# Two small setup tiles of a decode block, written by ScalarE copies instead of by GpSimd

## The chip, the cores and the metric

The kernel runs on one core of a Trainium2 chip. The metric is device time in microseconds (us) of one execution, the median of several. A core has TensorE (PE, matmuls; its weight loads are listed as PEld), VectorE (DVE), ScalarE (ACT), GpSimd (POOL), and SyncE (SP), which here only issues DMAs. The engines run side by side, each through its own list of instructions in order, and wait for each other on semaphores. DMAs are issued from SP's list and from ACT's list (the rows marked SPq and ACTq).

## The reference

One token (`x`, 1024 numbers) goes through a layernorm, then through two branches whose results are added to `x`: attention over the last 4096 positions of a key and value cache (32 query heads, 4 key/value heads of 128), and a second layernorm with a two-layer MLP of 3584 hidden units.

```python
xn = _layernorm(x)
q = (xn @ wq).reshape(B, Sq, Hq, Dh).transpose(0, 2, 1, 3)
k, v = last W=4096 positions of each cache, repeated 8 times over the heads
p = _softmax(einsum(q, k) * Dh ** -0.5)
A = einsum(p, v).reshape(B, Sq, Hq * Dh) @ wo
B = gelu(_layernorm(xn) @ w1 + b1) @ w2 + b2
return x + A + B
```

All inputs are bf16. With one token every matrix is read once and used for a matrix-vector product: 4 MB each of K, V (windows) and 8 MB each of wq and wo, some 7 MB each of w1 and w2, together close to 40 MB.

## The kernel before, in words

The order of the work on each engine follows from the program's order; a framework adds the semaphore waits that the tiles' reads and writes ask for.

**The stream of loads.** SP issues nearly all of them, in this order: the four K groups into the first half of the `big` tile `kq` (line 76), the two halves of wq (line 85), half of b1 (204), w1 (207), four V groups (214), w2 (220), and wo in five pieces (228), the last of them 256 KB. The tiles live in pools of two buffers each: `big` holds `kq`, `kt2`, `w1t`, `w2t` in turn, `ring` holds the second half of wq, `v_sb`, and the two halves of wo. So the load of w1 waits for the readers of `kq`, that of w2 for the readers of `kt2`, and the last four pieces of wo for the readers of `v_sb`. ACT issues four tiny loads at the start (108 to 111): `x` in two layouts, b2, and half of b1.

**Setup.** POOL fills constants: `zb` (line 91, bf16: an identity, one-hot selections `spread`, `sel_x`, `sel_b`, and room for the query), `ones_f`, `mhalf`, then `zf` (line 113, float32: 512 columns of zeros named `zeros`, a selection `sel4` of 32 columns, and two columns `sel01`), then `o8z` (116) and further selections, made by affine_select, which puts a one where an index expression is met. ACT copies the identity to float32 (`ident_f`, line 96), loads its exp table, issues the four tiny loads, and copies `zeros` into the accumulators in PSUM: `accf` (178) and the two halves of `accq` (182).

**Layernorms.** PE spreads `x` over 128 partitions with `spread` as weights (145). Each of the two layernorms is a chain: two ACT passes with sums (153, 154), one PE sum over partitions (156), one ACT scaling (158), five small POOL steps (160 to 167). The first gives `xnT` (173), the second `yT`.

**The middle.** DVE transposes K (191), DVE and ACT move its blocks (202, 200); PE makes q (237), the hidden layer (249), the scores (266) and the values' sum `o_all` (302).

**The end.** The final product adds 28 rows of w2 and 32 rows of wo. All but the last eight go to `accf` as single rows (329; for wo the weights are `o8z[:, c, 1:2]`, one column). ACT copies `accf` to `bulk` (333). Then two small accumulators `acct` collect the output in its final layout: first the bulk is moved over with selections as weights (342; one of the four selections is `sel01`, a 33x2 matrix whose only one stands in row 0, column 1), then the last eight rows of wo are added with two-column weights (348), of which one column is the attention output and the other must be zero: `o8z` has three columns a row, and `o8z[:, c, 1 - r:3 - r]` takes (value, zero) or (zero, value). Line 313 writes the middle column late; the outer two must hold zeros from the setup. `res` is put together by DVE (351) and ACT (352) and sent out by SP and ACT (354, 355).

In the listed program `tc.issue_after(instruction)` puts what is in its block behind that instruction in the engine's order.

Of the kernel before, what the change touches and what calls it, by code (L numbers as in the profile page):

```python
# [10 lines left out]
ALU = mybir.AluOpType  # L11
# [4 lines left out]
def kernel(  # L16
# [14 lines left out]
    nc = tc.nc  # L31
# [15 lines left out]
    CWO = NQ // P  # L47
# [34 lines left out]
    for i in range(2):  # L82
# [11 lines left out]
                            pattern=[[-1, P]], channel_multiplier=1)  # L94
    ident_f = consts.tile([P, P], FP32)
# [11 lines left out]
    with tc.issue_after(first_exp.ins):  # L107
# [5 lines left out]
    nc.gpsimd.memset(zf[:], 0.0)  # L113
    zeros = zf[:, 0:512]
    o8z = consts.tile([P, CWO, 3], BF16)
    nc.gpsimd.memset(o8z[:], 0.0)
    sel4 = zf[:, 512:512 + Hq]
    sel01 = zf[0:33, 512 + Hq:]
    nc.gpsimd.affine_select(out=sel01, in_=sel01, compare_op=ALU.not_equal, fill=1.0, base=-1,
                            pattern=[[1, 2]], channel_multiplier=2)  # L120
    qm_f = zb[:, P:P + 160]
    spread = zb[0:Hq, 288:800].rearrange("h (q p) -> h q p", q=4)
    sel_b = zb[0:8, 800:1056].rearrange("k (s m) -> k s m", s=2)
# [1 line left out]
    for sel, base in ((sel_x, 0), (sel_x, -64), (sel_b, 0)):  # L125
        nc.gpsimd.affine_select(out=sel, in_=sel, compare_op=ALU.not_equal, fill=1.0, base=base,
                                pattern=[[-16, 2], [-1, sel.shape[2]]], channel_multiplier=16)
    for R in range(4):
        nc.gpsimd.affine_select(out=sel4, in_=sel4, compare_op=ALU.not_equal, fill=1.0, base=-32 * R,
                                pattern=[[-1, Hq]], channel_multiplier=1)  # L130
# [3 lines left out]
                            pattern=[[-1, 4], [1, P]], channel_multiplier=-4)  # L134
# [4 lines left out]
                            pattern=[[-REP, Hkv]], channel_multiplier=1)  # L139
    nc.gpsimd.affine_select(out=gmask[:], in_=gmask[:], compare_op=ALU.is_ge, fill=0.0, base=REP - 1,  # L140
                            pattern=[[REP, Hkv]], channel_multiplier=-1)
# [38 lines left out]
    acch = ps_acc.tile([P, 2, 512], FP32, tag="acch", name="acch")  # L180
    for b in range(2):
        nc.scalar.copy(out=accq[:, b, :], in_=zeros)
    for s in range(2):
        nc.tensor.matmul(accf[0:64, 256 * s:256 * s + 256], lhsT=sel_x[:, s, :], rhs=xb8[:], start=(s == 0), stop=False)

# [46 lines left out]
    for i, w3 in enumerate(wq_tiles):  # L232
        for r in range(4):
            c = 4 * i + r
# [151 lines left out]
```

## Time and profile before

| what | value |
|---|---|
| three runs | 101.68, 101.80, 101.92 us; median 101.80 |
| the profiled execution's own time | 101.61 us |
| its span, first to last instruction | 99.5 us (so 2.1 us lie around it) |
| mean granted TensorE clock | 0.914 |
| busy: PE, DVE, ACT, POOL | 47.6, 37.5, 28.9, 8.9 us |
| moved by DMA | 39.91 MB, mean 401 GB/s over the span |

How to read it: busy times of engines are averages over stages with different limits, so they say little by themselves. The chain of waits goes back from the last instruction, at each step to what released it. In the timeline a row gives start, duration, engine and line, the tile written, an arrow, the tile read, and in brackets the idle time of that engine before it with what ended it. Lines over 356 belong to the wrapper that all engines run before and after the program.

### The profile page before, as it was taken

How to read it: one execution, taken by the hardware profiler on the slowest of the kernel's cores; microseconds unless marked ns; L12 is line 12 of the kernel's file. 1: busy time of each engine (PE TensorE's matmuls, PEld its weight loads, DVE VectorE, ACT ScalarE, POOL GpSimd, SP SyncE). 2: the span in 40 equal slices, each digit the busy share in tenths (PEclk: the TensorE clock that was granted, in tenths of full speed). 3: DMA queues.
4: the chain of work that ended last, by engine and by line, in shares of the span. 5: the costliest groups of instructions: out<-in, count | busy, mean ns of one | idle time of the engine just before them, and what ended most of it. 6: DMA issues, size and time to landing. Idle time of an engine off the chain costs nothing.

```text
span 99.5 us, 1001 instructions
## 1 busy us (share of the span) xinstructions
PE 47.6 (48%) x405; PEld 20.2 (20%) x405; DVE 37.5 (38%) x25; ACT 28.9 (29%) x32; POOL 8.9 (9%) x35
## 2 busy tenths in 40 slices
PE   0005110007600880089139807999100999895770
PEld 0003110002100310063036402334000333341240
DVE  0079999999999970010613015000600000000001
ACT  5306200007999999900150080000010000000201
POOL 7921560000000000000001000000000000000000
PEclk9999999999999999999999985579955558999999
DMA  2999999999999888999499999899899999899930
GB/s 46 389 409 435 484 428 474 474 422 422 448 422 581 369 369 369 392 669 415 181 425 422 435 576 392 369 576 491 369 392 418 422 422 422 362 441 408 394 114 1
DMA packets 2539, 39.91 MB, mean 401 GB/s; under 512 B 340, under 2 KB 360, under 8 KB 616
## 3 DMA queue, kind: packets, MB, share of 16 engines
q1 hardware_dynamic: 2460, 39.85, 93.9%
q8 instruction: 3, 0.05, 0.2%
q10 hardware_dynamic: 76, 0.01, 0.1%
HBM read 39.86 MB, written 0.00 MB: 401 GB/s over the span
## 4 chain that ended last, share of the span: by engine, by line
DMA 79%; PE 14%; SPq 3%; issue 1%; DVE 0%; DVEq 0%
DMA v_sb<-in_A_v_cache_dram 32%; DMA wo<-in_A_wo_dram 25%; DMA kq<-in_A_wq_dram 17%; PE o_all L302 10%; DMA kq<-in_A_k_cache_dram 5%; PE accq L237 4%; SPq L214 1%; SPq L228 1%; SPq L207 0%; PE acct L348 0%; DVE res L351 0%; DVEq L351 0%
## 5 line engine op out<-in xcount | busy, mean ns | idle before, releaser
L200 ACT COPY kt<-kt 32x4096 bf16<-32x4096 bf16 x5 | 18.0, 3601 | 10.2 <-DVE kt L191 10.2
L191 DVE STREAM_TRANSPOSE kt<-kq 128x4096 bf16<-128x4096 bf16 x4 | 17.4, 4413 | 5.6 <-DMA kq<-in_A_k_cache_dram 5.6
L202 DVE COPY kt<-kt 32x4096 bf16<-32x4096 bf16 x11 | 13.4, 1218 | 0.2
L302 PE MATMUL o_all<-v_sb,w1t 128*32 128x512 bf16 x32 | 9.8, 480 | 3.4 <-DMA v_sb<-in_A_v_cache_dram 3.4
L329 PE MATMUL accf<-w2t 128*1 128x512 bf16 x56 | 8.9, 496 | 4.8 <-DMA w2t<-in_B_w_dram 4.8
L351 DVE TENSOR_TENSOR res<-acct,bulk 34x120 bf16<-34x120 f32 x1 | 0.3, 275 | 25.1 <-PE acct L348 25.1
L237 PE MATMUL accq<-kq,xnT 128*1 128x512 bf16 x32 | 3.6, 625 | 10.2 <-DMA kq<-in_A_wq_dram 10.2
L333 ACT COPY bulk<-accf 34x512 f32<-34x512 f32 x1 | 0.6, 579 | 20.9 <-PE accf L329 20.9
L237 PE MATMUL accq<-wq,xnT 128*1 128x512 bf16 x32 | 3.6, 627 | 6.1 <-DMA wq<-in_A_wq_dram 6.1
L329 PE MATMUL accf<-wo,o8z 128*1 128x512 bf16 x48 | 5.5, 379 | 1.6 <-DMA wo<-in_A_wo_dram 1.6
L237 PEld LDWEIGHTS <-xnT 128*1 128x1 bf16 x64 | 2.1, 115 | 20.6 <-issue 20.6
L302 PEld LDWEIGHTS <-w1t 128*32 128x32 bf16 x32 | 3.7, 117 | 9.4 <-issue 7.4
L329 PEld LDWEIGHTS <-w2t 128*1 128x1 bf16 x56 | 3.0, 103 | 10.3 <-issue 8.6
L249 PE MATMUL acch<-w1t,yT 128*1 128x448 bf16 x64 | 5.1, 488 | 0.0
L305 DVE TENSOR_TENSOR o_m<-o_all,grs 32x512 f32<-32x512 f32 x1 | 0.7, 679 | 9.1 <-PE o_all L302 9.1
L297 DVE STREAM_TRANSPOSE w2t<-w1t 128x896 bf16<-128x896 bf16 x1 | 1.7, 1702 | 6.2 <-ACT w1t L294 6.2
L145 PE MATMUL x_ps<-x,zb 32*128 32x8 bf16 x4 | 0.2, 163 | 7.9 <-DMA x<-in_A_x_dram 7.9
L309 ACT CAST o_bf<-o_f 32x128 bf16<-32x128 f32 x1 | 0.3, 297 | 12.6 <-DVE o_f L307 12.6
L266 PE MATMUL sp<-kt,zb 128*32 128x512 bf16 x32 | 3.7, 631 | 0.3 <-DVE zb L258 0.3
L253 PE MATMUL qT_ps<-zb,w1t 128*128 128x128 bf16 x8 | 1.0, 311 | 5.2 <-ACT w1t L239 5.2
L293 POOL TENSOR_SCALAR zcol<-l_loc 128x1 f32<-128x1 f32 x1 | 0.2, 238 | 36.9 <-ACT w1t L281 36.9
L249 PEld LDWEIGHTS <-yT 128*1 128x1 bf16 x64 | 3.1, 108 | 1.5
(80 smaller groups left out, 40.6 us busy)
## 6 DMA issues: line engine op xcount, KB each, us to landing
w1t<-in_B_w_dram SPq DMA_DIRECT2D x1, 7168.0 KB, 24.0
w2t<-in_B_w_dram SPq DMA_DIRECT2D x1, 7168.0 KB, 29.8
kq<-in_A_k_cache_dram SPq DMA_DIRECT2D x4, 1024.0 KB, 7.1
kq<-in_A_wq_dram SPq DMA_DIRECT2D x1, 4096.0 KB, 17.2
wq<-in_A_wq_dram SPq DMA_DIRECT2D x1, 4096.0 KB, 24.3
v_sb<-in_A_v_cache_dram SPq DMA_DIRECT2D x4, 1024.0 KB, 25.9
wo<-in_A_wo_dram SPq DMA_DIRECT2D x1, 4096.0 KB, 39.1
wo<-in_A_wo_dram SPq DMA_DIRECT2D x1, 2048.0 KB
```

The source lines that it names most:

```text
L191: nc.vector.transpose(out=scr[:, g, :], in_=k2[:, g, :])
L200: nc.scalar.copy(out=dst, in_=src)
L202: nc.vector.tensor_copy(out=dst, in_=src)
L214: nc.sync.dma_start(out=v4[:, g, :, :], in_=A_v_cache[0, g, Sk - W:Sk, :].rearrange("(p c) d -> p c d", p=P))
L228: nc.sync.dma_start(out=tv[:, a:b, :], in_=wo_v[:, nr * i + a:nr * i + b, :])
L237: nc.tensor.matmul(accq[32 * t:32 * t + 1, b, :], lhsT=xnT[:, c:c + 1], rhs=w3[:, r, j * 512:(j + 1) * 512], start=(c == 0), stop=(c == C ...
L249: nc.tensor.matmul(acch[32 * t:32 * t + 1, b, :NH], lhsT=yT[:, c:c + 1], rhs=w1v[:, c, j * NH:(j + 1) * NH], start=False, stop=(c == C - 1 ...
L253: nc.tensor.transpose(qT_ps[:, b * 4 + hh, :], q_sb[:, b, hh * Dh:(hh + 1) * Dh], ident)
L266: nc.tensor.matmul(sp[32 * R:32 * R + 32, a, :], lhsT=qm[:, g, :], rhs=kT[:, g, c0:c0 + 512], start=(g == 0), stop=(g == Hkv - 1), tile_po ...
L297: nc.vector.transpose(out=hT, in_=h_sb.rearrange("p (d c) -> p c d", c=CW2))
L302: nc.tensor.matmul(o_all[:].rearrange("h g d -> h (g d)"), lhsT=eTb[:, 32 * c:32 * c + 32], rhs=v4[:, :, c, :], start=(c == 0), stop=(c == ...
L329: last = nc.tensor.matmul(accf[32 * half:32 * half + 1, :], lhsT=vec[kind](c), rhs=wap[:, half * 512:(half + 1) * 512], start=False, stop= ...
```

## The change

Two GpSimd instructions go: the memset of all 96 columns of `o8z`, and the affine_select that makes `sel01`. Two ScalarE copies come, placed in the program behind the copies of `zeros` into `accq`: one copies column 0 of the float32 identity (33 rows: a one in row 0, zeros below) into column 1 of `sel01`, whose column 0 is zero from the memset of `zf`; the other copies 96 of the float32 `zeros` into `o8z`, which makes them bf16. The tiles, their sizes and their readers stay.

```diff
@@ -113,11 +113,8 @@
     nc.gpsimd.memset(zf[:], 0.0)
     zeros = zf[:, 0:512]
     o8z = consts.tile([P, CWO, 3], BF16)
-    nc.gpsimd.memset(o8z[:], 0.0)
     sel4 = zf[:, 512:512 + Hq]
     sel01 = zf[0:33, 512 + Hq:]
-    nc.gpsimd.affine_select(out=sel01, in_=sel01, compare_op=ALU.not_equal, fill=1.0, base=-1,
-                            pattern=[[1, 2]], channel_multiplier=2)
     qm_f = zb[:, P:P + 160]
@@ -180,6 +177,8 @@
     for b in range(2):
         nc.scalar.copy(out=accq[:, b, :], in_=zeros)
+    nc.scalar.copy(out=sel01[:, 1:2], in_=ident_f[0:33, 0:1])
+    nc.scalar.copy(out=o8z[:].rearrange("p c f -> p (c f)"), in_=zeros[:, 0:3 * CWO])
     for s in range(2):
```

## The prediction

> **What bounds the kernel now.** I read the page's shares first, then the chain that ended last, and only then the timeline of the first 16 us, where the change lies.
>
> ```profile
> span 99.5 us, 1001 instructions
> PE 47.6 (48%) x405; PEld 20.2 (20%) x405; DVE 37.5 (38%) x25; ACT 28.9 (29%) x32; POOL 8.9 (9%) x35
> HBM read 39.86 MB, written 0.00 MB: 401 GB/s over the span
> DMA 79%; PE 14%; SPq 3%; issue 1%; DVE 0%; DVEq 0%
> ```
>
> No engine is busy for half of the span; DMA holds 79% of the chain, and neither POOL nor ACT appears in it. In order of time the chain is:
>
> ```profile
> 0.79 4.83 DMA kq<-in_A_k_cache_dram
> ...
> 5.64 17.23 DMA kq<-in_A_wq_dram
> ...
> 22.91 3.61 PE accq L237 x25
> ...
> 28.35 31.80 DMA v_sb<-in_A_v_cache_dram
> ...
> 60.29 9.78 PE o_all L302 x32
> ...
> 71.41 25.20 DMA wo<-in_A_wo_dram
> ...
> 96.65 0.33 PE acct L348 x8
> ...
> 97.03 0.28 DVE res L351
> ```
>
> The reader is to see that from 0.79 to 96.61 us the chain is loads, with two stretches of matmuls whose end lets SP issue more loads, and a tail of some 3 us. Setup is on none of it. The question is therefore only whether the two moved steps can push something onto this chain, or were holding it by a path that the chain doesn't show.
>
> **The change part by part.** Here is the setup in the timeline, from which all slacks below come.
>
> ```profile
> 2.82 0.17 POOL L116 MEMSET o8z<- 128x96 bf16 x1
> 2.96 0.28 POOL L126 TENSOR_SCALAR_AFFINE_SELECT zb<-zb 8x128 bf16<-8x128 bf16 x1
> 3.20 0.18 POOL L119 TENSOR_SCALAR_AFFINE_SELECT zf<-zf 33x2 f32<-33x2 f32 x1
> 3.34 0.65 POOL L126 TENSOR_SCALAR_AFFINE_SELECT zb<-zb 8x256 bf16<-8x256 bf16 x2
> 3.77 0.32 ACTq L111 DMA_DIRECT2D b<-in_B_b_dram  x1
> 4.13 0.59 ACT L178 COPY accf<-zf 128x512 f32<-128x512 f32 x1 [1.35 <-POOL zb L126]
> 4.80 0.10 PEld L145 LDWEIGHTS <-zb 32*128 32x128 bf16 x1 [4.80 <-POOL zb L133]
> 7.93 0.24 PE L145 MATMUL x_ps<-x,zb 32*128 32x8 bf16 x4 [7.93 <-DMA x<-in_A_x_dram]
> 9.31 0.17 ACT L158 ACTIVATE mv<-ln_tot 128x2 f32<-128x2 f32 x1 [0.19 <-PE ln_tot L156]
> 9.38 0.59 ACT L182 COPY accq<-zf 128x512 f32<-128x512 f32 x1
> 11.56 0.21 ACT L153 ACTIVATE cp<-xn_f 128x8 f32<-128x8 f32 x1 [1.59 <-POOL xn_f L167]
> 11.60 0.19 POOL L173 CAST xnT<-xn_f 128x8 bf16<-128x8 f32 x1
> 11.87 0.18 ACT L154 ACTIVATION_READ_ACCUMULATOR sq<-xn_f 128x1 f32 x1
> 12.73 0.17 ACT L158 ACTIVATE mv<-ln_tot 128x2 f32<-128x2 f32 x1 [0.68 <-PE ln_tot L156]
> 14.53 0.41 POOL L167 TENSOR_SCALAR yT<-cp,mv,rstd 128x8 bf16<-128x8 f32 x1
> ```
>
> *Removed from POOL.* The two instructions last 0.17 and 0.18 us, but POOL's instructions overlap a little: from the start of each to the start of the next is 2.96 - 2.82 = 0.14 and 3.34 - 3.20 = 0.14. So what follows on POOL comes 0.28 us earlier, at most 0.35 if the full durations count. What follows and matters is `spread`, for which the weight load of line 145 waits until 4.80: it would start at about 4.5. But the matmul behind it starts only at 7.93, released by the load of `x`. That load covers the gain: the slack of `spread` grows from 3.1 to 3.4 us, and nothing after 7.93 moves. The other POOL selections are used later still. POOL next works for the first layernorm behind ACT's scaling of 9.31. Gain on the path: 0; bounds 0 and 0.35.
>
> ACT's copy at 4.13 is put down to POOL's selection, yet ACT's own issue of the b1 load runs from 3.77 to 4.09; I take ACT's order as what held it. It too only has to be done before the ACT pass that follows `x_ps` at 7.93, so either reading gives 0.
>
> *Added to ACT, the `sel01` copy.* The program has it behind the copies into `accq`; in the instruction order of the changed kernel it stands between the scaling of the first layernorm (9.31) and the second copy into `accq` (9.38), and waits on ACT's own semaphore, for the identity made in the setup. A copy of 33x1 is not in the trace. The nearest rows:
>
> ```profile
> L102 ACT ACTIVATE dummy<-mhalf 1x1 f32<-1x1 f32 x1 | 0.2, 197 | 0.0
> L275 ACT COPY m_rep<-m_row 1x128 f32<-1x128 f32 x1 | 0.3, 297 | 7.2 <-DVE m_row L273 7.2
> L313 ACT CAST o8z<-o_ps 128x32 bf16<-128x32 f32 x1 | 0.2, 213 | 0.3 <-PE o_ps L312 0.3
> L96 ACT CAST ident_f<-zb 128x128 f32<-128x128 bf16 x1 | 0.3, 298 | 0.3 <-POOL mhalf L100 0.3
> ```
>
> One element takes 0.20 us, 128 take 0.30. With one element a partition I take 0.20; as ends 0.07 (the pitch from 9.31 to 9.38, if it overlaps as its neighbours do) and 0.30. Should its wait also drain the scaling in front, another 0.17 is possible. Behind it on ACT stands the second copy into `accq`, which then ends at 9.38 + 0.59 + 0.20 = 10.17, at worst 10.44, and behind that the first pass of the second layernorm at 11.56, which waits for POOL's `xn_f` anyway. So 1.1 us of idle ACT time cover it. POOL's step of the first layernorm needs the scaling, which stands ahead. On the path: 0. If that cover were gone, 0.20 us would pass to `yT` alone.
>
> *Added to ACT, the `o8z` copy.* In the changed order it stands behind the second pass and its accumulator read (11.87 + 0.18 = 12.05) and ahead of the second scaling (12.73), for which ACT sat idle 0.68 us waiting for PE. 96 elements lie between 32 (0.213) and 128 (0.298): 0.213 + 64/96 x 0.085 = 0.27 us, ends 0.21 and 0.30. It runs from 12.05 to 12.32 inside an idle gap that ends at 12.73 whatever ACT does. On the path: 0. With that cover gone as well, both copies would make `yT` late by 0.47: ready at 14.53 + 0.41 + 0.47 = 15.41. The users of the two layernorms:
>
> ```profile
> 22.91 3.58 PE L237 MATMUL accq<-kq,xnT 128*1 128x512 bf16 x32 [10.22 <-DMA kq<-in_A_wq_dram]
> 23.11 18.05 ACT L200 COPY kt<-kt 32x4096 bf16<-32x4096 bf16 x5 [10.20 <-DVE kt L191]
> 51.85 0.54 PE L249 MATMUL acch<-w1t,yT 128*1 128x448 bf16 x3
> 94.35 0.26 PE L342 MATMUL acct<-bulk,zf 33*2 33x120 f32 x1
> ```
>
> `yT` is first read at 51.85, 36 us later. `xnT` is ready at 11.79, isn't touched by the new copies, and is read at 22.91, when wq lands. ACT's next long work, the K blocks, starts at 23.11 behind DVE; the new copies are done some 10 us before.
>
> *Waits at the end.* `sel01` is read at 94.35 and now depends on ACT instead of POOL, but line 342 waits for ACT's `bulk` in any case, and the copy of `o8z`, done at 12.32, lies 58 us ahead of the end of `o_all` (60.29 + 9.78 = 70.07), behind which line 313 writes into it on the same engine. No wait is added there.
>
> *Queues.* No load is issued elsewhere or past another: ACT's four issues end at 4.09, ahead of both copies, and SP's list is untouched. Neither copy writes a tile that a load waits for.
>
> Sum: 0 (POOL) + 0 + 0 (ACT) + 0 (waits, queues) = 0 on the profiled execution's 101.61 us. That execution lies 0.19 under the median of the runs shown, so the forecast for a median is 101.80 us.
>
> *Is the stream of loads slowed by ACT's added work?* This is the one place where I can see a cost. The copies read and write the memory that the loads fill, in 0.47 us of new ACT time. Windows of the trace (TensorE, weight loads, DVE, ACT, POOL busy us and counts; clock; DMA share; GB/s):
>
> ```profile
> 8.00:10.00 2.00, 1.32 (x8) 0.76 (x7) 2.00 (x1) 1.57 (x7) 0.36 (x2) 1.00 0.98 416
> 10.00:12.00 2.00, 0.00 (x0) 0.00 (x0) 2.00 (x2) 0.44 (x4) 1.43 (x5) 1.00 1.05 442
> 40.00:42.00 2.00, 0.00 (x0) 0.00 (x0) 0.00 (x0) 1.98 (x2) 0.00 (x0) 1.00 1.06 459
> 44.00:46.00 2.00, 2.00 (x24) 1.23 (x20) 0.00 (x0) 0.00 (x0) 0.00 (x0) 1.00 1.06 459
> ```
>
> With ACT busy 1.57 us the loads ran at 416 GB/s, with 0.44 us at 442: 6% less for 1.13 us more of ACT. By that pair 0.47 us of copies would cost 0.47/1.13 x 0.06 x 2 us = 0.05 us. The other pair, ACT busy all the time and not at all, gives 459 both times, so 0. I take 0, because PE was busy in the first window too. The Trainium skill, "SBUF — State Buffer", section "SBUF: two separate sides", says that an engine's accesses and a DMA's use separate ports and can't slow each other; by it the cost is 0. The second pair of windows agrees with that rule, the first pair doesn't show it cleanly.
>
> **The rivals.** A time change of over 0.2% (0.2 us) is about what a measurement of this kernel can tell from none; the three runs shown span 0.24.
>
> *Faster, setup counts.* If the start of the program is on a path that the chain doesn't show, POOL's 0.28 us come off: 101.80 - 0.28 = 101.52. For it: the weight load of 145 did wait for POOL until 4.80. Against: the 3.1 us from 4.80 to 7.93 spent waiting for `x`, and 11 us between `xnT` and wq.
>
> *Slower, the copies stop the stream.* If loads stand still while ACT's copies write or read, the 0.47 us are lost where every microsecond of the stream counts: 101.80 + 0.47 = 102.27. Its place is 9.4 to 12.3 us, beside wq's load. It decides once the copies stop the loads for over 0.2 of their 0.47 us. For it: 416 against 442 GB/s. Against: 459 at full ACT load, and that ACT and POOL swap 0.35 us of POOL writes for it.
>
> *The stream falls otherwise.* The loads share queues, and a start shifted by tenths of a microsecond may order packets differently. Nothing in the rows gives it a sign; from the span of the runs I give it 0.24 us to either side, 101.56 or 102.04.
>
> *The change doesn't do what it says.* It would if the copies were put ahead of the load of `x` on ACT; in the changed order they aren't, and even then 0.47 us on a load that lands at 7.93 would only take that much from the 11 us between `xnT` and wq. The time would be 101.80, so it goes with the forecast.
>
> **How the numbers follow.** Everything hidden: 0.60, giving 101.80 and no change. Setup counts: 0.14. Copies stop the stream: 0.14. Stream falls otherwise: 0.12, of which 0.05 faster and 0.07 slower, since added work near the stream can rather hurt. So faster 0.19, same 0.60, slower 0.21. The range goes from the setup rival less half the runs' span, 101.52 - 0.12 = 101.40, up to the other rival's 102.27; the likeliest case alone has 101.6 to 102.0.
>
> **What the profile of the changed kernel would show.** Right: POOL's list without lines 116 and 119 and the weight load of `spread` at about 4.5, the matmul behind it still released by the load of `x` near 7.9; a `sel01` copy of some 0.2 us near 9.4, an `o8z` copy of some 0.27 near 12.1, the second scaling still released by PE; the q matmuls still released by wq near 22.9; the last chain again loads, ending near 96.6. Wrong: any POOL or ACT step of the setup in the chain; the q matmuls released by `xnT`; a lower GB/s in 8 to 13 us with the same loads landing later; or a tail at lines 342 or 348 that waits for ACT. If the landing of wq, V or wo differs while all of the setup is hidden, the time moved through the stream, and my sum missed a term there.

## The result, and the profile after

The changed kernel takes 101.41 us (median of six, 101.30 to 101.67) against 101.91 us for the kernel before beside it: a ratio of 0.996, 95% interval 0.9949 to 0.9971. It is faster by 0.4%, twice what I had called measurable, and I had forecast no change. The range (101.4 to 102.27) holds the number at its very edge. Three executions of the kernel before in the sets of runs below took 106.5, 123.8 and 212.6 us, far above the rest, and are left out of every mean and ratio.

The profile doesn't show where the gain is. Its span is *longer* than before (99.8 against 99.5 us), and its execution, at 101.67 us, is the slowest of the six. The head of the page and the totals of the chain, of the changed kernel:

```profile
span 99.8 us, 1000 instructions
PE 46.0 (46%) x405; PEld 19.9 (20%) x405; DVE 37.5 (38%) x25; ACT 29.1 (29%) x34; POOL 8.6 (9%) x33
DMA 80%; PE 13%; SPq 3%; issue 1%; DVE 0%; DVEq 0%
```

The chain of the changed kernel in order of time (start, duration, what):

```profile
0.78 5.00 DMA kq<-in_A_k_cache_dram
...
5.79 17.09 DMA kq<-in_A_wq_dram
...
22.92 3.61 PE accq L236 x30
...
28.36 32.21 DMA v_sb<-in_A_v_cache_dram
...
60.71 8.73 PE o_all L301 x32
...
71.01 25.92 DMA wo<-in_A_wo_dram
...
96.97 0.33 PE acct L347 x8
...
97.35 0.27 DVE res L350
```

It is the chain of before, piece by piece: the first q matmuls start 0.01 us later, the last load lands 0.32 us later (71.01 + 25.92 = 96.93 against 96.61). The setup of the changed kernel in the timeline:

```profile
2.83 0.89 POOL L123 TENSOR_SCALAR_AFFINE_SELECT zb<-zb 8x128 bf16<-8x128 bf16 x3
4.52 0.10 PEld L142 LDWEIGHTS <-zb 32*128 32x128 bf16 x1 [4.52 <-POOL zb L130]
7.99 0.24 PE L142 MATMUL x_ps<-x,zb 32*128 32x8 bf16 x4 [7.99 <-DMA x<-in_A_x_dram]
9.37 0.17 ACT L155 ACTIVATE mv<-ln_tot 128x2 f32<-128x2 f32 x1 [0.19 <-PE ln_tot L153]
9.44 0.18 ACT L180 COPY zf<-ident_f 33x1 f32<-33x1 f32 x1
9.52 0.58 ACT L179 COPY accq<-zf 128x512 f32<-128x512 f32 x1
11.65 0.19 POOL L170 CAST xnT<-xn_f 128x8 bf16<-128x8 f32 x1
12.02 0.25 ACT L181 CAST o8z<-zf 128x96 bf16<-128x96 f32 x1
12.79 0.17 ACT L155 ACTIVATE mv<-ln_tot 128x2 f32<-128x2 f32 x1 [0.51 <-PE ln_tot L153]
14.58 0.41 POOL L164 TENSOR_SCALAR yT<-cp,mv,rstd 128x8 bf16<-128x8 f32 x1
22.92 3.58 PE L236 MATMUL accq<-kq,xnT 128*1 128x512 bf16 x32 [10.17 <-DMA kq<-in_A_wq_dram]
51.55 0.54 PE L248 MATMUL acch<-w1t,yT 128*1 128x448 bf16 x3
```

Everything forecast for the setup is there: `spread` ready at 4.52 instead of 4.80, the matmul behind it still released by the load of `x` (7.99), the second scaling still released by PE, the q matmuls still released by wq. `yT` is done 0.05 us later and read 36 us afterwards. So nothing in this pair of spans shows the 0.4%. That left the part which the profile's views don't show: an execution's time minus its own span. The two profiled executions have 101.61 - 99.5 = 2.1 us before and 101.67 - 99.8 = 1.9 us after the change.

### The profile page after: what moved, and what is told of

Same layout as the page of the kernel before. It is cut to its first block, busy times and chain, and to the rows that moved or that the text cites. A ratio compares the mean times of both kernels' runs of the same rounds, so it can differ in the third digit from the quotient of the medians.

```text
span 99.8 us, 1000 instructions
## 1 busy us (share of the span) xinstructions
PE 46.0 (46%) x405; PEld 19.9 (20%) x405; DVE 37.5 (38%) x25; ACT 29.1 (29%) x34; POOL 8.6 (9%) x33
## 4 chain that ended last, share of the span: by engine, by line
DMA 80%; PE 13%; SPq 3%; issue 1%; DVE 0%; DVEq 0%
DMA v_sb<-in_A_v_cache_dram 32%; DMA wo<-in_A_wo_dram 26%; DMA kq<-in_A_wq_dram 17%; PE o_all L301 9%; DMA kq<-in_A_k_cache_dram 5%; PE accq L236 4%; SPq L227 1%; SPq L213 1%; SPq L206 0%; PE acct L347 0%; DVE res L350 0%; DVEq L350 0%
## 5 line engine op out<-in xcount | busy, mean ns | idle before, releaser
L328 PE MATMUL accf<-w2t 128*1 128x512 bf16 x56 | 8.0, 454 | 5.7 <-DMA w2t<-in_B_w_dram 5.7
L301 PE MATMUL o_all<-v_sb,w1t 128*32 128x512 bf16 x32 | 8.7, 440 | 3.1 <-DMA v_sb<-in_A_v_cache_dram 3.1
L248 PE MATMUL acch<-w1t,yT 128*1 128x448 bf16 x64 | 6.0, 566 | 0.0
L248 PEld LDWEIGHTS <-yT 128*1 128x1 bf16 x64 | 3.6, 122 | 1.8
```

Of the source, the lines that this page charges most:

```text
L248: nc.tensor.matmul(acch[32 * t:32 * t + 1, b, :NH], lhsT=yT[:, c:c + 1], rhs=w1v[:, c, j * NH:(j + 1) * NH], start=False, stop=(c == C - 1 ...
L301: nc.tensor.matmul(o_all[:].rearrange("h g d -> h (g d)"), lhsT=eTb[:, 32 * c:32 * c + 32], rhs=v4[:, :, c, :], start=(c == 0), stop=(c == ...
L328: last = nc.tensor.matmul(accf[32 * half:32 * half + 1, :], lhsT=vec[kind](c), rhs=wap[:, half * 512:(half + 1) * 512], start=False, stop= ...
```

## The experiments

Every execution comes with its time and its span (in tenths), so "around the span" below is the mean of time minus span over a kernel's executions; the spread is their standard deviation. Results beside the kernel before on the same chip; POOL's list counts every instruction the program gives POOL, register moves, drains and semaphore steps too (the traces record one less in every kernel: 60 before, 57 in the changed one).

| kernel | POOL's list | executions | mean span | around the span (spread) | ratio, 95% |
|---|---|---|---|---|---|
| before (four sets of runs, three chips) | 61 | 20, 29, 32 and 30 | 99.66 to 99.72 | 2.12 to 2.13 (0.05) | 1 |
| changed | 58 | 6 | 99.65 | 1.78 (0.07) | 0.996, 0.9949 to 0.9971 |
| e0_before_again | 61 | 11 | 99.65 | 2.12 (0.06) | 0.9998, 0.9987 to 1.0008 |
| e6_after_again | 58 | 6 | 99.68 | 1.77 (0.06) | 0.9972, 0.9961 to 0.9984 |
| e1_o8z_alone | 60 | 11 | 99.63 | 1.98 (0.04) | 0.9984, 0.9974 to 0.9993 |
| e2_sel01_alone | 59 | 5 | 99.64 | 1.76 (0.05) | 0.9967, 0.9955 to 0.998 |
| e3_act_added | 61 | 11 | 99.60 | 2.14 (0.06) | 0.9994, 0.9983 to 1.0005 |
| e4_dve | 58 | 5 | 99.68 | 1.72 (0.03) | 0.9957, 0.9946 to 0.9969 |
| e7_pool_late4 | 65 | 12 | 99.68 | 1.89 (0.13) | 0.9978, 0.9966 to 0.9989 |
| e8_after_late3 | 61 | 11 | 99.68 | 2.12 (0.04) | 0.9998, 0.9987 to 1.001 |
| e9_after_late4 | 62 | 12 | 99.74 | 2.00 (0.03) | 0.9987, 0.9974 to 1.0 |
| e10_after_late6 | 64 | 12 | 99.71 | 1.86 (0.03) | 0.9971, 0.996 to 0.9983 |
| e11_after_late7 | 65 | 12 | 99.65 | 2.01 (0.07) | 0.9976, 0.9964 to 0.9989 |
| e12_pool_less2 | 56 | 10 | 99.74 | 1.77 (0.06) | 0.9967, 0.9952 to 0.9983 |
| e13_before_late3 | 64 | 12 | 99.72 | 1.92 (0.17) | 0.9984, 0.9968 to 1.0 |
| e14_after_late2 | 60 | 12 | 99.68 | 1.97 (0.05) | 0.9989, 0.998 to 0.9999 |
| e15_before_late16 | 77 | 9 | 99.67 | 1.80 (0.08) | 0.9968, 0.9957 to 0.9979 |
| e16_after_late5 | 63 | 10 | 99.64 | 1.76 (0.05) | 0.9966, 0.9954 to 0.9977 |

### Is the gain real, and which of the two steps has it?

The kernel before and the changed kernel were run again unchanged. For e1 only the zeros of `o8z` were moved, for e2 only `sel01`:

```diff
 # e1_o8z_alone, against before
-    nc.gpsimd.memset(o8z[:], 0.0)
...
+    nc.scalar.copy(out=o8z[:].rearrange("p c f -> p (c f)"), in_=zeros[:, 0:3 * CWO])
 # e2_sel01_alone, against before
-    nc.gpsimd.affine_select(out=sel01, in_=sel01, compare_op=ALU.not_equal, fill=1.0, base=-1,
-                            pattern=[[1, 2]], channel_multiplier=2)
...
+    nc.scalar.copy(out=sel01[:, 1:2], in_=ident_f[0:33, 0:1])
```

The kernel before again:

> The kernel before, unchanged, as a second program beside itself. Theory S (the setup's start is on a hidden path), theory O (the gain lies in the time around the span: the profiled executions have 101.61 - 99.5 = 2.1 us around the span before the change and 101.67 - 99.8 = 1.9 us after it) and theory V (any new build moves the time by some tenths): S and O expect a ratio of 1.000 +- 0.001, V allows 0.996 to 1.004 only if the build differs, so 1.000 too. What it must give besides: the span of each run of the kernel before, so that time and span can be set side by side. O expects spans near 99.6 and times near 101.9, so 2.2 us around the span; S expects spans near 100.0 and 1.8 us around it.

The changed kernel again:

> The changed kernel again, beside the kernel before on the same chip. S, O: ratio 0.995 to 0.997 as first measured. If the gain was a matter of that one chip or hour: 0.999 to 1.001.

`o8z` alone:

> Only o8z is zeroed by ACT, sel01 stays with POOL. S: POOL is 0.14 us earlier, half of the gain, ratio 0.998. O tied to POOL's instruction count: half or a step, 0.996 or 0.998. My prediction's sum: 1.000.

`sel01` alone:

> Only sel01 is made by ACT, o8z stays with POOL. S: POOL is 0.14 us earlier, ratio 0.998. O tied to the affine_select (an instruction of POOL that works another way than a memset): the whole gain here, 0.996, and none in the run with o8z alone. My prediction's sum: 1.000.

The gain is there again, in another set of runs (0.9972), and the same program beside itself gives 0.9998. The spans don't differ: 99.63 to 99.68 us on average in all four. The difference in time is the difference around the span: 2.12 to 1.77, 0.35 us. So theory O stands and theory S, the setup on a hidden path, has nothing left to explain. The two steps don't add up: `o8z` alone takes 0.14 us off, `sel01` alone takes all of the 0.35 off, both together no more.

### POOL's list, or ACT's?

```diff
 # e3_act_added, against before: both POOL steps stay
         nc.scalar.copy(out=accq[:, b, :], in_=zeros)
+    nc.scalar.copy(out=sel01[:, 1:2], in_=ident_f[0:33, 0:1])
+    nc.scalar.copy(out=o8z[:].rearrange("p c f -> p (c f)"), in_=zeros[:, 0:3 * CWO])
 # e4_dve, against before: VectorE does both
-    nc.gpsimd.memset(o8z[:], 0.0)
+    nc.vector.memset(o8z[:], 0.0)
...
-    nc.gpsimd.affine_select(out=sel01, in_=sel01, compare_op=ALU.not_equal, fill=1.0, base=-1,
-                            pattern=[[1, 2]], channel_multiplier=2)
+    nc.vector.tensor_copy(out=sel01[:, 1:2], in_=ident_f[0:33, 0:1])
 # e7_pool_late4, against before; e8_after_late3 the same with 3, against the changed kernel
     nc.gpsimd.tensor_scalar_mul(out=grs[:], in0=gmask[:], scalar1=rs[:])
+    for _ in range(4):
+        nc.gpsimd.memset(mhalf[:], -0.5)
```

ACT's copies added, POOL untouched:

> The kernel before with the two ACT copies added and both POOL steps kept (each tile is written twice with the same values). So far the spans are equal (99.65 us on average before and after the change) and the time around the span differs: 2.12 before, 1.98 with o8z alone, 1.76 with sel01 alone, 1.78 with both. Theory P (the time around the span grows with the number of POOL's instructions, whatever they do): ratio 1.000, 2.12 around the span. Theory A (ACT's longer list makes it shorter): 0.996 to 0.997, 1.75 around. The setup theory S: 1.000 and the span unchanged.

The steps moved to DVE:

> Both steps go from POOL to DVE instead of ACT: DVE zeroes o8z and copies the identity's column into sel01. P: POOL's list is as short as in the changed kernel, so 0.9965 and 1.77 us around the span. A: ACT's list is as before, so 1.000 and 2.12. A copy of DVE between two transposes may cost some 0.1 us of the transposes, which the loads hide.

The kernel before, four idle POOL instructions more:

> The kernel before with four 128x1 memsets more on POOL behind the second layernorm, where POOL then waits for over 30 us: nothing in the setup moves. P with a price of 0.1 to 0.2 us an instruction: 2.5 to 2.9 us around the span, ratio 1.004 to 1.008. P as a step that has already been taken: 2.12, ratio 1.000. S: 1.000, since the setup is untouched.

The changed kernel, three idle POOL instructions more:

> The changed kernel with three 128x1 memsets more on POOL behind the second layernorm, so that POOL's list has as many instructions as before the change, while the setup stays short. P: the gain is gone, ratio 1.000 and 2.1 us around the span. S: the setup is as short as in the changed kernel, so the gain stays, 0.9965. A third theory R (the affine_select that makes sel01 is special, it needs a register set ahead of it): the gain stays too, 0.9965 and 1.77 around the span.

Three instructions more on ACT's list make no difference (e3: 2.14, ratio 0.9994), and the gain is the same when VectorE takes the work over (e4: 1.72, ratio 0.9957). What counts is POOL's list: with three idle memsets more the changed kernel loses its whole gain (e8: 2.12, 0.9998). Its timeline shows that this is not the setup coming back:

```profile
2.84 0.89 POOL L123 TENSOR_SCALAR_AFFINE_SELECT zb<-zb 8x128 bf16<-8x128 bf16 x3
4.53 0.10 PEld L142 LDWEIGHTS <-zb 32*128 32x128 bf16 x1 [4.53 <-POOL zb L130]
7.72 0.24 PE L142 MATMUL x_ps<-x,zb 32*128 32x8 bf16 x4 [7.72 <-DMA x<-in_A_x_dram]
14.33 0.42 POOL L164 TENSOR_SCALAR yT<-cp,mv,rstd 128x8 bf16<-128x8 f32 x1
14.68 0.41 POOL L290 MEMSET mhalf<- 128x1 f32 x3
```

`spread` is ready at 4.53 as in the changed kernel; the three memsets lie at 14.68, where POOL has nothing else to do until about 51 us. A steady price per instruction, which I had named as one form of theory P, falls with e7: four instructions more than before make it *faster* (0.9978).

### By length, or by content?

For e9, e10, e11, e14 and e16 the changed kernel got 4, 6, 7, 2 and 5 late memsets; for e13 and e15 the kernel before got 3 and 16 (the edit of e7 with another count). For e12 the list of the changed kernel was made shorter:

```diff
 # e12_pool_less2, against the changed kernel, in the layernorm
-        var = small.tile([P, 1], FP32, tag="ln_var")
-        nc.gpsimd.tensor_tensor(out=var[:], in0=mv[:, 1:2], in1=msq[:], op=ALU.subtract)
         ve = small.tile([P, 1], FP32, tag="ln_ve")
-        nc.gpsimd.tensor_scalar(out=ve[:], in0=var[:], scalar1=eps, scalar2=None, op0=ALU.add)
+        nc.gpsimd.tensor_scalar(out=ve[:], in0=mv[:, 1:2], scalar1=msq[:], scalar2=eps, op0=ALU.subtract, op1=ALU.add)
```

Length 62:

> The changed kernel with four late POOL memsets: POOL's list has 62 instructions (moves, drains and semaphore steps counted). So far, by that length: 58 and 59 give 1.72 to 1.78 us around the span, 60 gives 1.98, 61 gives 2.12 to 2.14 (three kernels), 65 gives 1.89, scattered from 1.69 to 2.07. Theory L (the length alone decides, as a place in a block of the list, so up and down): between 2.13 and 1.89 or higher, a smooth row with its neighbours. Theory C (the kind of instruction counts, and the late memsets are only waiting time): no order by length.

Length 64:

> The changed kernel with six late POOL memsets, length 64. L with a block of 8 instructions: the same as length 56, which runs beside it. L with a block of 64: the row turns between 62 and 66. C: no order by length.

Length 65:

> The changed kernel with seven late POOL memsets, length 65, as the kernel before with four had. L: the same 1.89 us around the span with the same scatter, ratio 0.998. C, or the setup theory: another value, since the setup here is the changed kernel's.

Length 56:

> The changed kernel with one POOL step less in each layernorm: the difference of the mean square and the square, and the addition of eps, in one instruction. POOL's list has 56 instructions, no other engine's list changes. L without a block (shorter is better): 1.5 to 1.7 us around the span, ratio 0.994 to 0.996. L with a floor: 1.75, ratio 0.9965, as the changed kernel. L with a block of 8: the same as length 64.

Length 64 from the kernel before:

> The kernel before with three late POOL memsets: length 64 with the setup of before. Theory L (length alone): 1.86 us around the span as the changed kernel with six had, so ratio 0.997, faster than before by adding useless work. Theory C (content): anything else, most simply 2.13 and 1.000, since the setup is that of the kernel before.

Length 60 from the changed kernel:

> The changed kernel with two late POOL memsets: length 60, as the kernel with o8z alone moved had. L: 1.98 us around the span, ratio 0.9985. C: 1.77, ratio 0.9965, since the setup is the changed kernel's.

Length 63:

> The changed kernel with five late POOL memsets: length 63, between 62 (2.00) and 64 (1.86). L: 1.86 to 2.00 around the span, ratio 0.997 to 0.9985. C: no order.

Length 77:

> The kernel before with sixteen late POOL memsets: length 77 = 61 + 16. L with a block of 8 or 16: 2.13 around the span, ratio 1.000. L as a single hump near 61: 1.7 to 1.9, ratio 0.996 to 0.998. A steady price for each instruction: over 2.13.

In order of length the time around the span is:

```
56    58              59    60          61                    62    63    64          65          77
1.77  1.78 1.77 1.72  1.76  1.98 1.97   2.12 2.12 2.14 2.12   2.00  1.76  1.86 1.92   1.89 2.01   1.80
```

Where several kernels share a length, up to 64, they agree within 0.06 us, whatever the instructions are: 60 was reached with `o8z` moved and with two idle memsets, 61 with the old setup, with ACT's copies added, and with the short setup and three idle memsets. (At 64 the second value is a mean that one execution at 2.46 pulls up; its median is 1.88.) So theory C falls, and theory L holds near 61, as a hump: 61 costs some 0.35 us, its neighbours on both sides about 0.2, and 63 is back at the floor. Three things don't fit a simple row. At 64 the time is up again by 0.1 us, in both kernels. At 65 the two kernels differ by 0.12 us and scatter (1.69 to 2.07 in e7). And nothing repeats: 77, which is 61 + 16, has 1.80, and 56 and 64 differ by 0.1, so a block of 8 or of 16 instructions is excluded as the rule.

The plainest case is e13, by the timeline of its setup:

```profile
2.83 0.17 POOL L116 MEMSET o8z<- 128x96 bf16 x1
3.21 0.18 POOL L119 TENSOR_SCALAR_AFFINE_SELECT zf<-zf 33x2 f32<-33x2 f32 x1
4.81 0.10 PEld L145 LDWEIGHTS <-zb 32*128 32x128 bf16 x1 [4.81 <-POOL zb L133]
14.68 0.41 POOL L291 MEMSET mhalf<- 128x1 f32 x3
```

It has the old setup, both steps on POOL, `spread` at 4.81, and three useless instructions on top; its median is 101.61 us against 101.82 beside it (the interval of the ratio reaches up to 1.0).

No variant beats the changed kernel: e2, e4, e12, e15 and e16 lie at the same floor of 1.72 to 1.80 us around the span.

Where the extra time lies is shown in part. The profile's views end with the last instruction, but the traces go on recording semaphore increments for some 2 us behind it. In the profiled executions of the kernels with 56, 58, 60, 61 and 63 instructions the last nine increments lie at the same places, from 1.55 us behind the span to 1.91, within 0.01 us (at 59 and 77 all nine are 0.09 us later). At 62 the last three are 0.24 us late (2.06 instead of 1.82, and so on); in both kernels of 64 the last seven are 0.14 us late (1.76 instead of 1.62). The time around the span of these executions, 1.99 us at 62 and 1.86 and 1.85 at 64, is 0.27 and 0.14 us above the 1.71 and 1.72 of e4, e6, e12 and e16. So at 62 and 64 the loss lies behind the span. In both kernels of 65 a block of 51 increments begins some 0.35 us late (at 1.15 and 1.16 us instead of 0.81), but the last nine come on time.

At 60 and 61 no increment is late, so where their 0.2 and 0.35 us lie is not shown; the increments ahead of the span follow no order by length. The place of the delay comes earlier as the list grows from 62 to 64 to 65, as if POOL stopped at one place in its stream of instructions which moves through the end of the program. Loads of instructions may be what it waits for: besides three loads of 16 KB that every trace has, there is one of 8 KB at 18.7 us of the span in e15 (length 77) and one 1.8 us behind the span in e11 (65), and in no other trace from the span's start on. But e7 has no such load at the same length 65, and no run tests this reading. Why a list of 61 costs most stays open.

## Why the prediction was wrong

**Wrong: the base of the sum.** "Sum: 0 ... on the profiled execution's 101.61 us" took those 101.61 us as a span that the change could move plus a rest that it couldn't. Every term was worked out for the span. The 2.1 us around it got no term, no bound and no rival, which puts their change at zero without a reason, and the whole effect sits there: they fell to 1.77 us, by 0.35, because POOL's list went from 61 to 58 instructions (e8 takes the gain back by putting three idle ones in). In the "Removed from POOL" step, "Gain on the path: 0; bounds 0 and 0.35" is right for the span and silent on the rest. The 0.35 there are durations in the setup and have nothing to do with the measured 0.35.

**Right, by the spans: nothing in the span moves.** The mean spans of the kernel before (99.66 to 99.72) and of the changed one (99.65, 99.68) agree within what they scatter. The prediction's last sign of being wrong, a load that lands at another time with the setup hidden, was met in the profiled pair (0.32 us later), but it pointed to the stream of loads, and the equal mean spans show no gain there.

**Right: the POOL step.** `spread` came to 4.52 (forecast about 4.5), and the load of `x` covered it.

**Right: the two ACT copies.** Their groups in the changed kernel's profile (busy us, mean ns, idle before):

```profile
L181 ACT CAST o8z<-zf 128x96 bf16<-128x96 f32 x1 | 0.3, 254 | 0.0
L180 ACT COPY zf<-ident_f 33x1 f32<-33x1 f32 x1 | 0.2, 177 | 0.0
```

They take 0.25 and 0.18 us, forecast 0.27 and 0.20, at the places forecast and under the cover that was named: ACT still waits 0.51 us for PE behind the `o8z` copy. The `sel01` copy overlaps its neighbours and sets the one behind it back by 0.08 us (9.44 to 9.52), near the low end of 0.07.

**Right: the loads aren't slowed by ACT's copies.** The first two windows of the changed kernel answer to the two shown of before (columns as there). The `o8z` copy runs behind them, so the third window is given too, with that of before in the last row:

```profile
8.00:10.00 2.00, 1.38 (x8) 0.82 (x7) 2.00 (x1) 1.54 (x8) 0.30 (x2) 1.00 1.02 429
10.00:12.00 2.00, 0.00 (x0) 0.00 (x0) 2.00 (x2) 0.48 (x5) 1.49 (x5) 1.00 1.01 426
12.00:14.00 2.00, 0.59 (x2) 0.58 (x3) 2.00 (x1) 0.44 (x4) 0.71 (x4) 1.00 1.42 610
...
12.00:14.00 2.00, 0.59 (x2) 0.58 (x3) 2.00 (x1) 0.23 (x2) 0.76 (x4) 1.00 1.30 557
```

429 and 426 GB/s where before had 416 and 442, with ACT about as busy in each: nearly the same sum (855 and 858), so the 6% between the two windows of before were not ACT's doing. From 12 to 14 us ACT works 0.21 us more and the loads run at 610 GB/s instead of 557, not slower. In e3, with the copies added to everything else, the mean span is 99.60. That agrees with what the Trainium skill, "SBUF — State Buffer", section "SBUF: two separate sides", states: engines and DMAs reach this memory by separate ports.

**The rivals.** "Faster, setup counts" gave 101.52 and lies near the measured 101.41, but for the wrong reason: e8 has the short setup and no gain, e13 the long setup and some of it. That the range holds 101.41 is luck: its lower end, 101.40, was set by this rival. "Copies stop the stream" falls with e3. "The stream falls otherwise" may be what spreads the spans of one and the same program (99.3 to 100.1 us for the kernel before), but it isn't the gain.

**The chances.** 0.60 for no change rested on the cover inside the span alone. A case "something that the profile doesn't show" had no share.

## What to carry to other kernels

A time has two parts, the span that the profile shows and a rest around it; where a change is worth less than one percent, compare the means of both parts over many executions before looking for a cause in the trace. Here the rest moved by 0.35 us with the number of instructions on GpSimd's list, up and down, whatever they did: a small gain from taking out an instruction may be gone with the next edit, and the test for it is to put idle instructions of the same number back. One profiled execution is no witness for half a percent: the pair shown here had the faster kernel with the longer span.

## What the runs showed of the hardware that was not expected

In this kernel the time around the span depends on the length of POOL's instruction list: 1.72 to 1.78 us for 56, 58, 59 and 63 instructions, 1.97 to 2.00 for 60 and 62, 2.12 to 2.14 for 61, in kernels with different contents. Three instructions more on ACT's list (e3, a wait among them) or two more on DVE's (e4) had no such effect; no other lengths of those lists were run. At 62 and 64 the traces show the delay behind the last instruction: the last semaphore increments come 0.24 and 0.14 us late. Here, moving an instruction off POOL, or adding an idle one, was thus worth up to 0.35 us of 101.8 without any change in the span.
